# Seven products for the second MLP layer of batch 0, with the w2 sums and batch 1's scaling rearranged around them

## The chip, the cores and the metric

The kernel runs on one core of one Trainium2 chip. A core has TensorE (PE, matrix multiplication; PEld is its loading of weights), VectorE (DVE), ScalarE (ACT) and GpSimd (POOL); SyncE (SP) issues DMA transfers, as POOL does for the weights. The metric is the device time of one execution in microseconds.

## The reference, cut to what matters

```python
# retention, q, k, v: (4, 8, 768, 64); gamma of head h: 1 - 2**(-5 - h)
for t in range(S):
    state = gamma * state + k[:, :, t] (outer) v[:, :, t]
    y[:, :, t] = D**-0.5 * q[:, :, t] @ state
x = y, heads side by side                      # (4, 768, 512)
# mixer
h = x.transpose(0, 2, 1) @ U @ V               # over the 768 tokens, rank 32
u = x + h.transpose(0, 2, 1)
ch = np.maximum(u @ w_ch1, 0.0) @ w_ch2        # 512 -> 2048 -> 512
out = u + ch
```

Inputs and output are fp32; the matmuls here run in bf16.

## The kernel before, in words

For each of four batches the kernel computes retention by chunks of 128 tokens (six chunks), the low-rank mixing, a first MLP layer (512 to 2048, relu) and a second one (2048 to 512). The MLP of batch b and the retention of batch b+1 are woven together: `weave` walks a list of slots (pieces of the two layers, TensorE work of 0.43 to 0.65 us each) and, ahead of each slot, runs the side work that `put` has hung on its number. Every engine executes its instructions in the order in which this program issues them, so the slot numbers fix each engine's queue. `n1` is the number of slots in the first layer (32).

First layer: `mlp1(b, m, hf)` makes one 128-row block m (of 16) of the hidden activation for half hf of the tokens (384 columns), and evicts it with a relu to `gTs[b]`, mostly on ScalarE (L121).

Second layer: batches 1 to 3 use seven products in place of eight (Strassen's scheme) on 2 x 2 blocks. Hidden blocks 0-7 and 8-15 (`lo`, `hi`) and the two token halves give a11, a12, a21, a22; w2's quadrants are b11, b12, b21, b22. `g_sums` (L599) makes five sums of activation blocks on VectorE, `w2_sum` (L589) five of weights (three into `w2s`, two in place). `product` (L620) runs one product for one of three token blocks i: 8 matmuls of 256 columns in two slots, the names in the order 4 5 1 2 3 7 6, accumulated in three PSUM groups A (4, 2, 6), B (5, 3), C (1, 7). `after` (L649) adds the results to `res`: ScalarE copies the partial results of 4, 5, 1 and 2 out of PSUM, POOL makes five sums of them (s5, u1, s1, u2 and later c21), VectorE adds 3, 7 and 6 from PSUM.

Batch 0 instead has `mlp2` (L566): for each of six token chunks one bank, one matmul of V with P and 16 matmuls of 512 columns over all hidden blocks in eight slots, then one add of x on VectorE and one store.

Retention of batch 1, woven into batch 0's second layer: `ret_in` (L275) scales k and q on POOL into `kd` and `qd` (`ret_k`, `ret_q`, L257 and L262) and, for chunks 2 to 4, issues loads of batch 2. `ret_T` (L417) transposes both on TensorE (L424) into one bank and evicts it; `ret_S` makes the scores (two banks for a chunk) and masks them on VectorE (L446); `ret_O` (L450) makes output and state. `at[c]` is the slot of chunk c's transposes, and `ret_in` of c is issued `lead` slots earlier. `mix_P`, `mix_n` (`mix_r` on VectorE, a cast on ScalarE, a DMA transpose) and `mix_u` then make batch 1's mixed input uT, which its first layer reads; they hang on `mix_at`.

The first loads of batch 1 (`gate`) are held back by a small ScalarE instruction in slot 14, so that they come after the weights.

## Time and profile before

| | us |
|---|---|
| median of 3 timed runs (lowest, highest) | 225.2 (224.98, 225.26) |
| the profiled execution's own time | 224.54 |
| its span, first to last instruction | 222.8 |
| PE busy, of the span | 213.7 |
| batch 0, first layer (PE, from the timeline) | 27.43 to 48.31 |
| batch 0, second layer with batch 1's retention | 48.31 to 82.28 |
| VectorE busy / ScalarE busy / POOL busy | 128.1 / 124.9 / 94.2 |

How to read the rows further down. A timeline row has its start, its length, the engine, the line of the kernel, the operation, output<-input, shapes and a count of merged instructions; in brackets stand the engine's idle time ahead of it and what ended it. A matmul's length includes its way through the array, so rows overlap, and the rate is read from start to start. A row of stretches has the stretch, its length, the busy time (and instructions) of PE, PEld, DVE, ACT and POOL, then PE's granted clock, the DMA share and GB/s. A row of a tile or line has its shortest, median and longest duration in ns and its first and last start.

### The profile page before, as it was taken

Reading aid. Unit: us, or ns where it says so; the run is one execution under the profiler, and the core shown is the slowest. Engines: PE = TensorE matmul, PEld = TensorE weight load, DVE = VectorE, ACT = ScalarE, POOL = GpSimd, SP = SyncE. Lnnn points to the kernel's source line nnn. Section 1 sums busy time; section 2 is a strip of 40 time slices with the busy share of each in tenths; the row PEclk is TensorE's granted clock in tenths of the full one; section 3 lists DMA queues with packets and bytes.
Section 4 is the critical chain, followed back from the end, with each engine's and each line's share of the span. In section 5 each row is a group of like instructions: output and inputs, shape, how many; then the busy total and the mean of one; then the engine's idle time right before and its main releaser. Section 6 shows DMA issues by size and latency. Waiting matters only on the chain.

```text
span 222.8 us, 4880 instructions
## 1 busy us (share of the span) xinstructions
PE 213.7 (96%) x1920; PEld 143.3 (64%) x1927; DVE 128.1 (57%) x249; ACT 124.9 (56%) x256; POOL 94.2 (42%) x110
## 2 busy tenths in 40 slices
PE   7898999999999999999999999999999999999991
PEld 2466756554565555566887766657787866668881
DVE  8587640036776456789983721868974423555113
ACT  3377757762327356777445727767454657772220
POOL 6756920039752530614506099423605320006650
PEclk9999999999999999999999999999999999999998
DMA  6999999999999998969499969978621571000222
GB/s 168 245 265 190 154 188 205 199 210 219 201 222 251 228 238 186 222 143 147 94 190 213 234 125 239 179 160 145 83 97 46 121 125 40 0 3 0 94 99 94
DMA packets 100774, 34.89 MB, mean 157 GB/s; under 512 B 87152, under 2 KB 97808, under 8 KB 100752
## 3 DMA queue, kind: packets, MB, share of 16 engines
q1 hardware_dynamic: 94640, 30.29, 66.1%
q0 software_dynamic: 6112, 4.29, 13.1%
q8 instruction: 15, 0.25, 0.5%
q14 instruction: 7, 0.06, 0.1%
HBM read 27.46 MB, written 6.29 MB: 152 GB/s over the span
## 4 chain that ended last, share of the span: by engine, by line
PE 78%; DMA 10%; POOL 3%; DVE 2%; ACT 2%; issue 1%; SPq 1%; POOLq 0%; DVEq 0%; ACTq 0%
PE bk L116 75%; DMA k_n<-in_k_dram 5%; DMA in<-in_q_dram 3%; DMA uT<-x 2%; POOL qd L311 1%; PE bk L424 1%; POOL qd L262 1%; DVE res L661 1%; ACT st L299 1%; POOL s L661 1%; PE bk L318 1%; DVE a L352 1%; POOL kd L306 0%; SPq L166 0%; ACT gT L121 0%
## 5 line engine op out<-in xcount | busy, mean ns | idle before, releaser
L116 PE MATMUL bk<-uT,w1b 128*128 128x384 bf16 x512 | 85.2, 326 | 0.4 <-DMA uT<-x 0.4
L121 ACT ACTIVATE gT<-bk 128x384 bf16<-128x384 f32 x123 | 60.1, 490 | 29.3 <-PE bk L116 29.3
L116 PEld LDWEIGHTS <-w1b 128*128 128x128 bf16 x512 | 49.8, 98 | 33.5 <-issue 0.8
L116 PEld LDWEIGHTS <-gT 128*128 128x128 bf16 x392 | 36.5, 98 | 14.4 <-issue 1.2
L116 PE MATMUL bk<-w2b,gT 128*128 128x256 bf16 (+1 forms) x234 | 43.0, 314 | 0.6 <-ACT s L657 0.2
L257 POOL TENSOR_TENSOR kd<-k_n,Gk 128x512 bf16<-128x512 f32 x18 | 21.7, 1205 | 47.2 <-DMA k_n<-in_k_dram 41.1
L661 POOL TENSOR_TENSOR s<-s,s 128x256 f32<-128x256 f32 x18 | 13.1, 728 | 61.1 <-ACT s L657 55.9
L608 DVE TENSOR_TENSOR gs<-gT 128x768 bf16<-128x768 bf16 x36 | 20.4, 604 | 21.6 <-ACT gT L121 21.3
L446 DVE TENSOR_TENSOR a<-bk,mask 128x512 bf16<-128x512 f32 x36 | 22.7, 682 | 3.8 <-PE bk L116 3.8
L661 DVE TENSOR_TENSOR res<-bk,res 128x256 f32<-128x256 f32 x28 | 10.7, 419 | 21.5 <-PE bk L116 17.0
L262 POOL TENSOR_TENSOR qd<-q_n,Gq 128x512 bf16<-128x512 f32 x18 | 20.3, 1129 | 5.4 <-DMA qkT<-qd 3.6
L116 PEld LDWEIGHTS <-gs 128*128 128x128 bf16 x216 | 20.5, 98 | 3.1
L116 PE MATMUL bk<-w2b,gs 128*128 128x256 bf16 x144 | 19.7, 273 | 0.0
L116 PE MATMUL bk<-w2s,gT 128*128 128x256 bf16 (+1 forms) x152 | 18.5, 267 | 0.0
L657 ACT ACTIVATE s<-bk 128x256 f32<-128x256 f32 x27 | 10.1, 381 | 15.0 <-PE bk L116 14.8
L463 ACT ACTIVATE x<-bk 128x512 bf16<-128x512 f32 x18 | 10.7, 595 | 12.5 <-PE bk L116 9.5
L594 DVE TENSOR_TENSOR w2s<-w2b 128x2048 bf16<-128x2048 bf16 x3 | 5.2, 1783 | 17.1 <-DMA w2b<-in_moe_w_ch_dram 17.1
L533 DVE TENSOR_TENSOR res<-bk,x 128x512 f32<-128x512 f32 x18 | 11.7, 685 | 4.9 <-PE bk L116 4.9
L608 DVE TENSOR_TENSOR gT<-gT 128x768 bf16<-128x768 bf16 x24 | 13.9, 620 | 0.0
L661 POOL TENSOR_TENSOR res<-res,s 128x256 f32<-128x256 f32 x18 | 13.1, 725 | 1.4
L538 ACT ACTIVATE x<-res 128x512 bf16<-128x512 f32 x15 | 9.2, 628 | 6.5 <-DVE res L533 6.2
L482 DVE TENSOR_TENSOR state<-bk,bmask 128x512 bf16<-128x512 f32 x15 | 10.4, 690 | 2.7 <-PE bk L116 2.5
(99 smaller groups left out, 230.9 us busy)
## 6 DMA issues: line engine op xcount, KB each, us to landing
out_dram<-res SPq DMA_DIRECT2D x23, 256.0 KB, 2.7
k_n<-in_k_dram SPq DMA_DIRECT2D x22, 256.0 KB, 4.7
v_n<-in_v_dram SPq DMA_DIRECT2D x22, 256.0 KB, 4.9
q_n<-in_q_dram SPq DMA_DIRECT2D x18, 256.0 KB, 4.9
w2b<-in_moe_w_ch_dram POOLq DMA_DIRECT2D x4, 512.0 KB, 15.2
in<-in_q_dram SPq DMA_DIRECT2D x3, 512.0 KB, 6.3
w1b<-in_moe_w_ch_dram POOLq DMA_DIRECT2D x4, 256.0 KB, 5.5
w1b<-in_moe_w_ch_dram POOLq DMA_DIRECT2D x2, 512.0 KB, 8.6
```

Source lines behind the costliest of these rows:

```text
L116: nc.tensor.matmul(o, l, r, **kw)
L121: nc.scalar.activation(o, i, AF.Relu if relu else AF.Copy)
L257: eng.tensor_tensor(kd, k_n, Gk[:, c].unsqueeze(2).to_broadcast([P, H, D]), op=ALU.mult)
L262: eng.tensor_tensor(qd, rc[b, c]["q_n"], Gq[:, c].unsqueeze(2).to_broadcast([P, H, D]), op=ALU.mult)
L446: nc.vector.tensor_tensor(r["a"][:, e], r["s"][e].rearrange("p (n t) -> p n t", n=NP), mask4, op=ALU.mult)
L463: nc.scalar.activation(x_of(b, c), o, AF.Copy)
L482: nc.vector.tensor_tensor(sb, ps.rearrange("p (n t) -> p n t", n=NP), bmask4, op=ALU.mult)
L533: nc.vector.tensor_tensor(res_of(b, j), h, xs[b, j], op=ALU.add)
L538: nc.scalar.activation(xs[b, j], res[b, j], AF.Copy)
L608: nc.vector.tensor_tensor(o, x, y, op=op)
L657: nc.scalar.activation(t[nm], o, AF.Copy)
L661: eng.tensor_tensor(o, x, y, op=op)
```

## The change

Batch 0's second layer now runs as the seven products too, and `mlp2` is gone. For this:

- The six products of V with P (`mix_r(0, j)`) move into batch 0's first layer, slots 4 to 15.
- The first layer of batch 0 makes hidden blocks in the order 0, 1, 8, 9, 2, 3, 10, 11, and so on; w1's pieces and w2's four pieces are loaded in that order of use.
- `g_sums(0, n)` come at slots 9, 17, 25 and at the layer's end. `w2_sum` works on halves (four hidden blocks of eight) and makes all ten sums in batch 0: five at slot 22, two at slot 30, three at the layer's end, between the last five activation sums. The two that stood in batch 1 are gone from there.
- Batch 1's scaling and transposes are hung on later slots (`at` = n1 + 11, 14, 18, 22, 26, 30, before n1 + 7, 12, 17, 22, 27, 32), its scores by single chunks, its mixing at n1 + 36 (of 42 slots, before n1 + 38 of 48).
- PSUM: batch 0's products use three banks; batch 1's first layer begins with four.

```diff
-    def mlp2(b, j, part, of):
-        if part == 0:
-            chp[b, j] = mm_bank()
-            matmul(chp[b, j], Vb[:, ts(j, P)], Ps[b], DM, start=True, stop=False)
-        ch = chp[b, j]
-        for m in range(part * NM // of, (part + 1) * NM // of):
-            matmul(ch, gTs[b][:, m, ts(j, P)], w2b[:, m], DM, start=False, stop=(m == NM - 1))
-        if part == of - 1:
-            o = res_of(b, j)
-            nc.vector.tensor_tensor(o, chp.pop((b, j)), xs[b, j], op=ALU.add)
...
-    def w2_sum(i):
-        b11, b12, b21, b22 = w2_quads()
-        o, x, y, op = ((w2s[:, 0], b11, b22, ALU.add), (w2s[:, 1], b11, b12, ALU.add),
-                       (w2s[:, 2], b21, b22, ALU.add), (b12, b12, b22, ALU.subtract),
-                       (b21, b21, b11, ALU.subtract))[i]
+    def w2_sum(i, h):
+        b11, b12, b21, b22 = (x[:, ts(h, HM // 2)] for x in w2_quads())
+        z = w2s[:, :, ts(h, HM // 2)]
+        o, x, y, op = ((z[:, 2], b21, b22, ALU.add), (b21, b21, b11, ALU.subtract),
+                       (z[:, 0], b11, b22, ALU.add), (z[:, 1], b11, b12, ALU.add),
+                       (b12, b12, b22, ALU.subtract))[i]
         nc.vector.tensor_tensor(o, x, y, op=op)
...
     def mlp1_slots(b):
         if b == 0:
-            return [lambda m=m, hf=hf: mlp1(b, m, hf) for m in range(NM) for hf in (0, 1)]
+            ms = [m + x for m in range(0, HM, 2) for x in (0, 1, HM, HM + 1)]
+            return [lambda m=m, hf=hf: mlp1(b, m, hf) for m in ms for hf in (0, 1)]
...
-            for i in range(3):
-                put(side, n1 + 1 + i, lambda i=i: w2_sum(i))
-            at, lead, mix_at = [n1 + 7 + 5 * c for c in range(NCK)], 4, n1 + 38
-            S_at = {(0, 1): n1 + 14, (2, 3): n1 + 24, (4,): n1 + 30, (5,): n1 + 35}
-            O_at = [n1 + i for i in (19, 22, 29, 32, 35, 38)]
+            for j, i in enumerate((4, 6, 8, 13, 14, 15)):
+                put(side, i, lambda j=j: mix_r(0, j))
+            for n, i in enumerate((9, 17, 25)):
+                put(side, i, lambda n=n: g_sums(0, n))
+            for i in range(5):
+                put(side, 22, lambda i=i: w2_sum(i, 0))
+            for i in (0, 1):
+                put(side, n1 - 2, lambda i=i: w2_sum(i, 1))
+            for f, *args in ((g_sums, 0, 3, (0, 1)), (w2_sum, 2, 1), (g_sums, 0, 3, (2,)),
+                             (w2_sum, 3, 1), (w2_sum, 4, 1), (g_sums, 0, 3, (3, 4))):
+                put(side, n1, lambda f=f, args=args: f(*args))
+            at, lead, mix_at = [n1 + i for i in (11, 14, 18, 22, 26, 30)], 4, n1 + 36
+            S_at = {(c,): n1 + i for c, i in enumerate((14, 17, 21, 25, 29, 33))}
+            O_at = [n1 + i for i in (18, 21, 25, 29, 33, 36)]
         if b == 1:
...
-            for n, i in enumerate((3, 4)):
-                put(side, 2 + 3 * n, lambda i=i: w2_sum(i))
...
         if b and nxt:
-            set_banks([0, 1, 2])
+            set_banks([0, 1, 2, TP])
+            put(side, 22, lambda: set_banks([0, 1, 2]))
...
-            put(side, mix_at, lambda: use.update(mix=[2, SA, SB, OB] if b == 0 else [SA, SB, OB]))
+            put(side, mix_at, lambda: use.update(mix=[SA, SB, OB] + [TP] * (b == 0)))
```

POOL's queue from the start of batch 0's second layer, before (kd_1_c and qd_1_c are the scaled k and q of batch 1's chunk c):

```order
L257 TENSOR_TENSOR kd_1_0_888<-k_n_1_0_730,Gk_157 128x512
L262 TENSOR_TENSOR qd_1_0_890<-q_n_1_0_733,Gq_156 128x512
L257 TENSOR_TENSOR kd_1_1_916<-k_n_1_1_736,Gk_157 128x512
L262 TENSOR_TENSOR qd_1_1_918<-q_n_1_1_738,Gq_156 128x512
L257 TENSOR_TENSOR kd_1_2_943<-k_n_1_2_740,Gk_157 128x512
L262 TENSOR_TENSOR qd_1_2_945<-q_n_1_2_742,Gq_156 128x512
```

And now (s4, s5, s1 and c21 are the copied partial results of products 4, 5, 1 and 2, res_0_j the output of batch 0's chunk j):

```order
L646 TENSOR_TENSOR s5_952<-s4_941,s5_952 128x256
L646 TENSOR_TENSOR res_0_0_669<-res_0_0_669,s5_952 128x256
L646 TENSOR_TENSOR s1_965<-s1_965,s5_952 128x256
L646 TENSOR_TENSOR res_0_3_744<-res_0_3_744,s1_965 128x256
L257 TENSOR_TENSOR kd_1_0_973<-k_n_1_0_752,Gk_157 128x512
L262 TENSOR_TENSOR qd_1_0_975<-q_n_1_0_755,Gq_156 128x512
L646 TENSOR_TENSOR res_0_3_744<-res_0_3_744,c21_981 128x256
L257 TENSOR_TENSOR kd_1_1_994<-k_n_1_1_758,Gk_157 128x512
L262 TENSOR_TENSOR qd_1_1_996<-q_n_1_1_760,Gq_156 128x512
```

Four sums of the first token block now stand ahead of chunk 0's scaling, and one more ahead of chunk 1's. On TensorE the transposes of chunk 0 stand after 11 of the 14 slots of that block.

VectorE's queue at the end of batch 0's first layer and behind it, before:

```order
L123 TENSOR_SCALAR gT_0_639<-bk6_55_655 128x384
L594 TENSOR_TENSOR w2s_191<-w2b_97 128x2048 x3
L576 TENSOR_TENSOR res_0_0_913<-bk1_84_877,x_0_0_395 128x512
L125 COPY qkT_1_1_939<-bk3_87_930 128x1024
L446 TENSOR_TENSOR a_1_0_975<-bk4_88_955,mask_175 128x512
```

and now:

```order
L578 TENSOR_TENSOR w2s_191<-w2b_97 128x1024
L578 TENSOR_TENSOR w2b_97<-w2b_97 128x4x256
L593 TENSOR_TENSOR gs_0_712<-gT_0_639 128x768 x2
L578 TENSOR_TENSOR w2s_191<-w2b_97 128x1024
L593 TENSOR_TENSOR gs_0_712<-gT_0_639 128x768
L578 TENSOR_TENSOR w2s_191<-w2b_97 128x1024
L578 TENSOR_TENSOR w2b_97<-w2b_97 128x4x256
L593 TENSOR_TENSOR gT_0_639<-gT_0_639 128x2x384 x2
L646 TENSOR_TENSOR res_0_0_669<-bk2_91_943,res_0_0_669 128x256
L646 TENSOR_TENSOR res_0_3_744<-bk2_91_943,res_0_3_744 128x256
```

Where three sums of w2 stood, there are now the last five half sums of w2 and the last five sums of the activation, in the order in which the products use them.

The end of batch 0's second layer on VectorE (res_1_j belongs to `mix_n` of batch 1's chunk j), before:

```order
L533 TENSOR_TENSOR res_1_3_1320<-bk4_116_1318,x_1_3_1224 128x512
L533 TENSOR_TENSOR res_1_4_1328<-bk5_117_1326,x_1_4_1268 128x512
L533 TENSOR_TENSOR res_1_5_1336<-bk6_118_1334,x_1_5_1291 128x512
L576 TENSOR_TENSOR res_0_5_1358<-bk0_115_1310,x_0_5_580 128x512
L125 CAST uT_1_1309<-bk6_122_1367 128x384
```

and now:

```order
L533 TENSOR_TENSOR res_1_3_1487<-bk5_125_1485,x_1_3_1340 128x512
L646 TENSOR_TENSOR res_0_5_803<-res_0_5_803,bk0_113_1305 128x256
L533 TENSOR_TENSOR res_1_4_1499<-bk6_126_1497,x_1_4_1413 128x512
L533 TENSOR_TENSOR res_1_5_1505<-bk3_127_1503,x_1_5_1449 128x512
L125 CAST uT_1_1470<-bk6_130_1521 128x384
```

The last add of batch 0's output now stands between the adds of chunks 3 and 4. On TensorE the matmuls for chunks 4 and 5 and for uT come behind the last slot; before, five slots lay between the first of them and the next layer.

More of the change, by code (lines that the diff above doesn't have):

```diff
@@ L822 @@
                          lambda: mlp1_two(0, (0, 1), 1), lambda: None]
-            for i, s in ((1, 2), (2, 3)):
-                put(side, i, lambda s=s: load_w1(512 * s, 512))
-            for s in range(4):
-                put(side, 4 + s, lambda s=s: load_w2(s))
+            for i, s in ((1, 512), (2, DH // 2 + 512)):
+                put(side, i, lambda s=s: load_w1(s, 512))
+            for n, s in enumerate((0, 2, 1, 3)):
+                put(side, 4 + n, lambda s=s: load_w2(s))
             for c, nm in ((0, "kq"), (1, "kq"), (2, "kq"), (0, "v"), (3, "kq"), (1, "v"), (4, "kq"),
```

30 lines of the change are left out of this document (12 added, 18 removed).

## The prediction

> **What bounds the kernel now.** I read first the page's busy shares, then the busy time by stretches, then TensorE's own timeline through batch 0.
>
> ```profile
> PE 213.7 (96%) x1920; PEld 143.3 (64%) x1927; DVE 128.1 (57%) x249; ACT 124.9 (56%) x256; POOL 94.2 (42%) x110
> 30.00:40.00 10.00, 10.00 (x63) 6.02 (x62) 0.56 (x1) 7.50 (x18) 0.00 (x0) 1.00 1.23 204
> 50.00:60.00 10.00, 9.41 (x76) 4.85 (x76) 7.58 (x9) 2.39 (x3) 9.07 (x8) 1.00 1.03 209
> ```
>
> PE is busy 96% of the span. In the stretches the columns are PE, PEld, DVE, ACT, POOL, then the granted clock. From 30 to 40 us VectorE and POOL stand almost empty; from 50 to 60 us POOL is busy 9.07 us of 10, and that is where the change puts more work on POOL.
>
> ```profile
> 27.43 21.05 PE L116 MATMUL bk<-uT,w1b 128*128 128x384 bf16 x128
> 48.31 0.38 PE L116 MATMUL bk<-P_sb,Vb 128*128 128x512 bf16 x1
> 52.14 0.40 PE L424 MATMUL bk<-ident,qd 128*128 128x128 bf16 x4 [0.43 <-POOL qd L262]
> ...
> 69.56 0.39 PE L424 MATMUL bk<-ident,qd 128*128 128x128 bf16 x4
> 70.00 0.39 PE L116 MATMUL bk<-state,qkT 128*128 128x128 bf16 x4
> 70.68 0.38 PE L116 MATMUL bk<-P_sb,Vb 128*128 128x512 bf16 x1
> 70.90 1.46 PE L116 MATMUL bk<-w2b,gT 128*128 128x512 bf16 x6
> 72.29 0.40 PE L116 MATMUL bk<-qkT 64*128 64x128 bf16 x8
> 72.62 0.40 PE L116 MATMUL bk<-state,qkT 128*128 128x128 bf16 x4
> 82.28 4.06 PE L116 MATMUL bk<-uT,w1b 128*128 128x384 bf16 x24
> ...
> 212.64 1.04 PE L116 MATMUL bk<-w2b,gs 128*128 128x256 bf16 x8
> 213.51 1.04 PE L116 MATMUL bk<-w2s,gs 128*128 128x256 bf16 x8
> ```
>
> Batch 0's first layer starts at 27.43, its second layer (with batch 1's retention woven in) at 48.31, batch 1's first layer at 82.28. The one wait of note in between is 0.43 us at 52.14: the first transposes of batch 1 waited for POOL's qd. Starts of neighbouring rows give unit costs: a 512-column matmul 0.22 us (70.68 to 70.90), a product's 8 matmuls of 256 columns 0.87 (212.64 to 213.51), the transposes T of a chunk 0.44 (69.56 to 70.00), its output part O 0.68 (70.00 to 70.68; chunks 0 and 5 do less, 0.46), its scores S 0.43 (six 512s from 70.90 end at 72.19; the next stage starts at 72.62). A slot of the second layer costs 0.43 in both kernels (2 x 512 or 4 x 256 columns).
>
> **PE's work.** The layer had 96 x 512 columns and gets 168 x 256: 96 x 0.2165 = 20.8 against 21 x 0.87 = 18.3, so **-2.5 us**. The six products with V stay, but move into the first layer: 6 x 0.22, so that layer ends at 48.31 + 1.3 = **49.6**. Their VectorE adds meet an engine that was idle there (0.56 us of work from 30 to 40 us), and cost nothing. Scores by chunk cost 6 x 0.43, about what two pairs and two singles took.
>
> **The sums on VectorE.** Their inputs first.
>
> ```profile
> L157 POOL DMA_DIRECT2D w2b<-in_moe_w_ch_dram x4: 777/792/805, 26.5 to 28.7; - x4
> DMA to landing us min/median/max: 12.3/15.2/19.1
> L594 DVE TENSOR_TENSOR w2b<-w2b x2: 1215/1216/1216, 84.3 to 85.4; 128x2048 bf16<-128x2048 bf16 x2
> L608 DVE TENSOR_TENSOR gs<-gT x36: 545/552/1393, 91.5 to 200.7; 128x768 bf16<-128x768 bf16 x36
> ```
>
> The last piece of w2 lands at 28.7 + 19.1 = 47.8. 2048 elements take 1.216 us and 768 take 0.55, so 1024 take about 0.68, with 0.6 from start to start. The sums over the first half of w2 and the third part of gT (five of 0.6, five of 0.47) run from 42 to 48 us beside the first layer. The next two half sums then run from 47.8 to 49.1, before product 4 reaches the second half of w2 at 50.0: covered. From the last eviction (50.3, 0.7 behind the last matmul) VectorE has four sums in a row (0.5 + 0.65 + 0.5 + 0.65) until 52.5, then three more. Product 3, due at 53.1, wants its half sum of b12 at 53.5; with POOL between (next part) it comes at 53.9: **+0.4**. Without the load of w2 in time (it would have to land 1 us later) product 4 would wait too; this is in the range. Batch 1 loses two w2 sums on VectorE, where nothing waited for them: nothing gained.
>
> **The scaling, behind the sums on POOL.** This is the main term. Durations:
>
> ```profile
> 213.77 0.38 ACT L657 ACTIVATE s<-bk 128x256 f32<-128x256 f32 x1 [0.49 <-PE bk L116]
> 214.23 0.72 POOL L661 TENSOR_TENSOR s<-s,s 128x256 f32<-128x256 f32 x1 [2.41 <-ACT s L657]
> ...
> 118.30 0.73 POOL L661 TENSOR_TENSOR s<-s,s 128x256 f32<-128x256 f32 x1 [6.43 <-ACT s L657]
> 119.10 0.73 POOL L661 TENSOR_TENSOR res<-res,s 128x256 f32<-128x256 f32 x1
> 119.79 0.72 POOL L661 TENSOR_TENSOR s<-s,s 128x256 f32<-128x256 f32 x1
> ...
> 131.85 1.04 POOL L257 TENSOR_TENSOR kd<-k_n,Gk 128x512 bf16<-128x512 f32 x1
> 132.85 1.04 POOL L262 TENSOR_TENSOR qd<-q_n,Gq 128x512 bf16<-128x512 f32 x1
> ```
>
> A POOL sum follows its product's end by 0.72 (product ends 213.51, POOL starts 214.23) and takes 0.75 from start to start; a scaling takes 1.00. In the new queue kd and qd of chunk 0 stand behind four sums of the first token block. Product 5 ends at 49.6 + 2 x 0.87 = 51.3, so POOL starts at 52.05, and qd is done at 52.05 + 4 x 0.75 + 2 x 1.0 = 57.1 if nothing disturbs it. Before, the two scalings started at 48.21, when k landed. What disturbs it:
>
> ```profile
> 47.98 1.23 DVE L594 TENSOR_TENSOR w2s<-w2b 128x2048 bf16<-128x2048 bf16 x1 [17.11 <-DMA w2b<-in_moe_w_ch_dram]
> 48.21 1.89 POOL L257 TENSOR_TENSOR kd<-k_n,Gk 128x512 bf16<-128x512 f32 x1 [18.70 <-DMA k_n<-in_k_dram]
> 49.12 2.06 DVE L594 TENSOR_TENSOR w2s<-w2b 128x2048 bf16<-128x2048 bf16 x1
> 50.08 2.01 POOL L262 TENSOR_TENSOR qd<-q_n,Gq 128x512 bf16<-128x512 f32 x1
> 51.11 2.06 DVE L594 TENSOR_TENSOR w2s<-w2b 128x2048 bf16<-128x2048 bf16 x1
> 52.05 2.02 POOL L257 TENSOR_TENSOR kd<-k_n,Gk 128x512 bf16<-128x512 f32 x1
> ```
>
> POOL's 1.04 becomes 2.0 and VectorE's 1.22 becomes 2.06, each as long as one of its own and one of the other's: while VectorE sums two SBUF tensors the two run by turns. So POOL's start waits for the sum that VectorE is in (until 52.5), and the last three VectorE sums (0.6 + 0.47 + 0.47) slip between POOL's: 57.1 + 0.45 + 1.5 = **59.0**.
>
> PE comes to chunk 0's transposes after 11 slots: 49.6 + 11 x 0.435 + 0.4 = 54.8. It waits **4.2 us** (2.7 without the turns, when product 3 doesn't wait either). The transposes sit in PE's queue ahead of the rest of product 7, so all products queue behind them. From there POOL's queue stays ahead of PE's by lateness: chunk 1 (one sum, two scalings) 59.0 + 2.75 = 61.75, PE there at 59.0 + 0.44 + 3 x 0.43 + 0.43 = 61.2: **+0.6**. Chunk 2 fits. Chunk 3's scaling stands behind two sums that need product 5 of the next block (copied at 64.95): 65.0 + 1.5 + 2.0 = 68.5, PE at 68.05: **+0.45**. Chunk 4 has three sums ahead: 68.5 + 2.25 + 2.0 = 72.75, PE at 68.5 + 0.44 + 3 slots + S + O + a slot = 71.8: **+0.9**. Chunk 5 fits (74.75 against 76.1). Loads are no part of it: k and q of chunk 0 land by 50.08 as before, the later ones are issued from the same queue position, and batch 2's loads, which follow chunks 2 to 4 on the DMA queue behind two output stores, are needed only in batch 1.
>
> **The tail.** Batch 1's mixing moves to the end of the layer.
>
> ```profile
> 78.57 2.06 DVE L533 TENSOR_TENSOR res<-bk,x 128x512 f32<-128x512 f32 x3 [1.61 <-PE bk L116]
> 79.29 1.99 ACT L538 ACTIVATE x<-res 128x512 bf16<-128x512 f32 x3 [1.93 <-DVE res L533]
> 81.19 1.44 ACT L121 ACTIVATE uT<-bk 128x384 bf16<-128x384 f32 x3
> 81.95 0.33 PE L116 MATMUL bk<-ident,x 128*128 128x128 bf16 x3
> ```
>
> Before, five slots of products lay between the mixing's matmuls and hid this chain: three adds on VectorE, three casts on ScalarE, and only behind them the evictions of uT that batch 1's first layer reads. In the new order two of the three adds' matmuls and all of uT's come after the last slot, at a time I call E. VectorE's adds then end at E + 0.46, + 1.5 and + 2.2 (a sum for the output in between), ScalarE's last cast at + 2.85, its first two uT evictions at + 3.3 and + 3.75. PE, done with the mixing at E + 1.75 (2 x 0.22 and 4 x 0.33, the row at 81.95), can start the second matmul of the layer only at + 3.8, so the layer runs as from + 3.65: **+1.9**. From qd of chunk 4 to E lie 11.3 us of PE work, so E = 84.05 and batch 1 starts as from 87.7, against 82.28. Of PE's idle time in the old kernel (222.8 - 213.7 = 9.1 us) 4.7 lie behind its last matmul and most of the rest before 27 us, so nothing later can give the shift back.
>
> **Sum.** -2.5 (columns) - 0.45 (the old wait) + 0.4 + 4.2 + 0.6 + 0.45 + 0.9 + 1.9 = **+5.5 us**. It is made against the profiled execution (224.54 us, its span 222.8); the median of the timed runs is 225.2, so I predict **230.7**.
>
> **Bounds.** Without the turns all from chunk 0 on comes 1.9 earlier: +3.6. With the tail's chain hidden, another 1.9 less: +1.7, the far low end. On the other side stands the clock.
>
> ```profile
> 1.19 6.27 PE L116 MATMUL bk<-idle 128*128 128x512 bf16 x18 [1.19 <-DVE idle L180]
> ...
> 218.00:219.00 1.00, 0.06 (x2) 0.00 (x0) 1.00 (x5) 0.00 (x0) 0.00 (x0) 1.00 0.08 27
> 220.00:221.00 1.00, 0.00 (x0) 0.00 (x0) 0.00 (x0) 0.00 (x0) 0.00 (x0) 0.87 0.95 318
> 221.00:222.00 1.00, 0.00 (x0) 0.00 (x0) 0.00 (x0) 0.00 (x0) 0.00 (x0) 0.50 0.12 33
> ```
>
> PE's last matmul ends at 218.06, and the granted clock falls to 0.50 at about 220.74 (0.87 of that microsecond): 2.7 us of an idle PE were enough once. And a cold start costs: the kernel's first 18 matmuls of 512 columns took 6.27 us where 18 x 0.2165 is 3.9.
>
> **Rivals.** *The clock falls in the new wait.* A gap of 4.2 us is longer than 2.7. At half speed the 2.17 us from 59.0 to chunk 1's transposes take 4.35 (2.2 lost; the start lost 2.4); they come at 63.35, not 61.75, and what follows on POOL follows PE: +1.6, so **232.3**. For it: the gap's length. Against: one gap only, and its length hangs on the turns. By the Trainium skill (TensorE: Matmul & The Clock Gate, "What's actually happening") the clock halves after a whole idle window of about 3.4 us in a free-running raster; by that rule a 4.2 us gap holds a whole window in one phase of four, my estimate. The trace's 2.7 us is shorter than the page's window.
>
> *The cheap case.* VectorE is done with its sums before POOL starts, so there are no turns: +3.6, **228.8**. It decides if VectorE ends by 52.05, 2 us earlier than its own work alone gives (54.1); nothing in the rows says so.
>
> *Not slower.* POOL's sums hold its queue for 0.35 us or less, the 0.72 being mostly latency that the next instruction overlaps. Then qd of chunk 0 is done at 52.05 + 1.4 + 2.0 = 55.45, PE waits 1.05 there, chunks 1 to 4 fit (ten sums and ten scalings take 13.5 us from 52.05, not 17.5 and the turns), and with the tail's 1.9 the change breaks even: **225.2**. Against it: POOL sums at 118.30, 119.10 and 119.79 started 0.80 and 0.69 apart, though copies for all of them were there.
>
> That the change moves nothing of this is excluded by POOL's order, in which the sums stand ahead of the scaling.
>
> **How the numbers follow.** The forecast has 0.52, the clock 0.25, the cheap case 0.18, not slower 0.05. The range takes in the first three with the low bound's tail in part: **228.0 to 233.0**; the forecast's own range is 229.5 to 231.5. A measurement of this kernel tells 0.2% from no change: faster 0.03, same 0.02, slower 0.95.
>
> **What would show it.** In the new profile: transposes of line 424 idle about 4 us for POOL's qd near 55 us; POOL rows of 0.72 grown to about 1.3 from 52 to 57; shorter waits at chunks 1, 3 and 4; a gap of about 2 us before batch 1's first layer, released by ScalarE's uT; PE's granted clock below 1.00 near 59 us or not. No POOL wait at the transposes, or a first layer of batch 1 that starts before 84 us, would prove the forecast wrong.

## The result and the profile after

| | before | after |
|---|---|---|
| median of 4 timed runs (lowest, highest), us | 225.23 (224.98, 225.77) | 231.26 (230.28, 231.46) |
| profiled execution: time / span / PE's mean granted clock | 224.54 / 222.8 / 0.995 | 230.28 / 228.5 / 0.986 |
| batch 0, second layer starts (PE) | 48.31 | 49.66 |
| batch 1, first layer starts (PE) | 82.28 | 87.93 |
| from there to the end of the span | 140.5 | 140.6 |

The changed kernel takes 1.0256 of the time before, 95% interval 1.022 to 1.0291. The last two rows of the table place the loss: it is complete when batch 1's first layer starts, and nothing behind that gives it back. A ratio compares fast runs alone: one run of e14 further down, 1.6% above the fastest of its kernel, counts as slow and is in that row's median but not in its ratio.

The profiled execution of the changed kernel, 230.28 us, is the fastest of its four (the others took 231.07 to 231.46). All rows below are from it, so about 1 us of the difference between the medians is in no row.

The page of the changed kernel: busy shares, and the ten microseconds in which POOL was nearly full before.

```profile
PE 215.0 (94%) x1997; PEld 151.2 (66%) x1999; DVE 143.2 (63%) x287; ACT 128.4 (56%) x267; POOL 102.6 (45%) x125
...
50.00:60.00 10.00, 6.40 (x55) 5.25 (x53) 6.38 (x10) 2.43 (x6) 7.76 (x9) 0.92 1.01 212
```

From 50 to 60 us PE works 6.40 of 10 us (9.41 before) at a mean clock of 0.92, VectorE 6.38 (2.39 before). Note that POOL shows *less* work than before, 7.76 against 9.07, because it now starts only when the first copies of products reach it; yet it is POOL that PE waits for. A busy share says nothing of when an engine is ready.

PE's timeline of the changed kernel, from product 3 to batch 1:

```profile
53.15 1.24 PE L116 MATMUL bk<-w2b,gT 128*128 128x256 bf16 x8
54.23 0.60 PE L116 MATMUL bk<-w2s,gT 128*128 128x256 bf16 x4
58.38 0.61 PE L424 MATMUL bk<-ident,qd 128*128 128x128 bf16 x4 [3.55 <-POOL qd L262]
...
62.22 0.40 PE L424 MATMUL bk<-ident,qd 128*128 128x128 bf16 x4
...
69.18 0.40 PE L424 MATMUL bk<-ident,qd 128*128 128x128 bf16 x4 [0.39 <-POOL qd L262]
73.36 0.40 PE L424 MATMUL bk<-ident,qd 128*128 128x128 bf16 x4 [0.70 <-POOL qd L262]
...
84.42 0.60 PE L116 MATMUL bk<-w2s,gT 128*128 128x256 bf16 x4
...
87.93 4.28 PE L116 MATMUL bk<-uT,w1b 128*128 128x384 bf16 x24 [0.55 <-ACT uT L121]
```

The four matmuls at 54.23 end their share of PE at 54.23 + 4 x 0.109 = 54.67, so the transposes of chunk 0 come 3.71 us late (the row's 3.55 counts from the modelled end of the last matmul, 0.16 later). The same 0.16 belongs to the other waits: 0.55 us at chunk 3, 0.86 at chunk 4. The last slot of the second layer ends at 84.42 + 0.44 = 84.86.

POOL's timeline of the changed kernel over the same stretch:

```profile
52.08 1.12 POOL L646 TENSOR_TENSOR s<-s,s 128x256 f32<-128x256 f32 x1 [22.41 <-DVE gs L593]
53.28 1.05 POOL L646 TENSOR_TENSOR res<-res,s 128x256 f32<-128x256 f32 x1
54.30 1.03 POOL L646 TENSOR_TENSOR s<-s,s 128x256 f32<-128x256 f32 x1
55.41 0.92 POOL L646 TENSOR_TENSOR res<-res,s 128x256 f32<-128x256 f32 x1
56.29 1.04 POOL L257 TENSOR_TENSOR kd<-k_n,Gk 128x512 bf16<-128x512 f32 x1
57.29 1.04 POOL L262 TENSOR_TENSOR qd<-q_n,Gq 128x512 bf16<-128x512 f32 x1
...
59.97 1.04 POOL L262 TENSOR_TENSOR qd<-q_n,Gq 128x512 bf16<-128x512 f32 x1
```

And VectorE's there:

```profile
51.93 0.69 DVE L578 TENSOR_TENSOR w2s<-w2b 128x1024 bf16<-128x1024 bf16 x1
52.65 1.10 DVE L578 TENSOR_TENSOR w2b<-w2b 128x1024 bf16<-128x1024 bf16 x1
53.67 2.07 DVE L593 TENSOR_TENSOR gT<-gT 128x768 bf16<-128x768 bf16 x2
55.67 0.41 DVE L646 TENSOR_TENSOR res<-bk,res 128x256 f32<-128x256 f32 x1
```

POOL's four sums stand ahead of chunk 0's scaling and take 1.12, 1.05, 1.03 and 0.92 us where one alone takes 0.72. VectorE's sums beside them grow as well: 1.10 for a half sum of w2, where the one that had started just ahead of POOL's first sum took 0.69, and 1.03 each for two that alone take 0.55. VectorE's add at 55.67, which reads PSUM, keeps its 0.41.

The clock of the changed kernel, microsecond by microsecond (the number behind POOL's busy time):

```profile
58.00:59.00 1.00, 0.62 (x7) 0.62 (x7) 0.00 (x0) 0.00 (x0) 1.00 (x3) 0.70 0.65 134
59.00:60.00 1.00, 1.00 (x8) 0.81 (x7) 0.00 (x0) 0.54 (x1) 1.00 (x3) 0.50 0.97 217
60.00:61.00 1.00, 1.00 (x7) 0.69 (x6) 0.42 (x1) 0.48 (x1) 1.00 (x3) 0.50 0.94 212
61.00:62.00 1.00, 1.00 (x9) 0.49 (x9) 0.01 (x1) 0.00 (x0) 1.00 (x3) 0.60 0.78 176
```

The clock fell just as PE resumed and stayed at half for (0.30 + 0.50 + 0.50 + 0.40) / 0.50 = 3.4 us. Chunk 1's transposes, for which POOL was ready at 61.0 (59.97 + 1.04), came at 62.22 with no wait.

### The profile page after: what moved, and what is told of

It reads as the page before. It is cut to its first block, busy times and chain, and to the rows that moved or that the text cites. A ratio compares the mean times of both kernels' runs of the same rounds, so it can differ in the third digit from the quotient of the medians.

```text
span 228.5 us, 5097 instructions
## 1 busy us (share of the span) xinstructions
PE 215.0 (94%) x1997; PEld 151.2 (66%) x1999; DVE 143.2 (63%) x287; ACT 128.4 (56%) x267; POOL 102.6 (45%) x125
## 4 chain that ended last, share of the span: by engine, by line
PE 63%; POOL 11%; issue 10%; DMA 4%; DVE 4%; ACT 3%; SPq 3%; POOLq 0%; DVEq 0%; ACTq 0%
PE bk L116 61%; POOL s L646 4%; POOL res L646 4%; DMA k_n<-in_k_dram 2%; POOL qd L262 2%; DMA q_n<-in_q_dram 2%; SPq L288 2%; POOL kd L257 1%; SPq L136 1%; PE bk L424 1%; DVE a L352 1%; ACT st L299 1%; DVE res L646 1%; ACT x L538 1%; ACT kT L299 1%
## 5 line engine op out<-in xcount | busy, mean ns | idle before, releaser
L646 POOL TENSOR_TENSOR s<-s,s 128x256 f32<-128x256 f32 x24 | 18.2, 758 | 87.5 <-ACT s L642 65.1
L593 DVE TENSOR_TENSOR gs<-gT 128x768 bf16<-128x768 bf16 x48 | 27.7, 614 | 20.8 <-ACT gT L121 20.3
L116 PEld LDWEIGHTS <-gs 128*128 128x128 bf16 x288 | 27.3, 98 | 3.9
L116 PE MATMUL bk<-w2b,gT 128*128 128x256 bf16 x192 | 26.4, 273 | 0.1
L116 PE MATMUL bk<-w2b,gs 128*128 128x256 bf16 x192 | 26.2, 273 | 0.0
L116 PE MATMUL bk<-w2s,gT 128*128 128x256 bf16 (+1 forms) x200 | 26.2, 277 | 0.0
L646 POOL TENSOR_TENSOR res<-res,s 128x256 f32<-128x256 f32 x24 | 17.9, 747 | 1.9
L593 DVE TENSOR_TENSOR gT<-gT 128x768 bf16<-128x768 bf16 x32 | 18.2, 609 | 0.0
L116 PE MATMUL bk<-w2s,gs 128*128 128x256 bf16 x96 | 12.6, 273 | 0.0
L116 PEld LDWEIGHTS <-qkT 64*128 64x128 bf16 (+1 forms) x204 | 8.4, 95 | 4.7 <-issue 2.9
```

The lines of the kernel that those rows point to most:

```text
L116: nc.tensor.matmul(o, l, r, **kw)
L593: nc.vector.tensor_tensor(o, x, y, op=op)
L646: eng.tensor_tensor(o, x, y, op=op)
```

## The experiments

They ran on four chips (e1, e4, e5, e6 on one; e7 to e10 on a second; e11 to e13 on a third; e14 on a fourth), each time with the kernel before beside them (medians 224.66 to 224.93 us). A ratio is to that kernel. The changed kernel itself was not repeated there; its 1.0256 is the mark, and as its interval is 1.022 to 1.0291, the ratios of e5 to e9 and of e13 are not clear of it: what these runs show is in their rows. "Start" is PE's first row of batch 1's first layer in the profiled run (before 82.28, changed kernel 87.93). Batch 0's first layer starts at 27.29 to 27.50 us in these profiles, so 0.2 us between two starts mean nothing.

| run | edit | median us | ratio, 95% | start |
|---|---|---|---|---|
| e1_scale_first | chunks 0 and 1 scaled ahead of the sums | 228.78 | 1.0178 (1.0155, 1.0202) | 86.29 |
| e4_tail | uT's evictions ahead of the casts | 232.10 | 1.0324 (1.0297, 1.0351) | 87.30 |
| e5_fill | 16 idle matmuls ahead of chunk 0's transposes | 229.45 | 1.0209 (1.0181, 1.0237) | 86.58 |
| e6_no_turns | last three VectorE sums left out | 229.52 | 1.0216 (1.0182, 1.0249) | 85.81 |
| e7_no_pool_sums | batch 0's POOL sums left out | 229.86 | 1.0208 (1.0143, 1.0273) | 87.96 |
| e8_rearranged | both kinds of sums reordered | 229.39 | 1.0220 (1.0155, 1.0286) | 86.83 |
| e9_tail_part | uT's evictions between the casts | 231.21 | 1.0286 (1.0249, 1.0324) | 86.74 |
| e10_no_sums | e6 and e7 together | 227.02 | 1.0113 (1.0055, 1.0171) | 85.07 |
| e11_adds_later | e8, with adds and sums in the order of use | 226.14 | 1.0059 (1.0030, 1.0088) | 82.77 |
| e12_and_mix_earlier | e11, mixing two slots earlier | 226.02 | 1.0060 (1.0041, 1.0078) | 82.94 |
| e13_mix_earlier | mixing two slots earlier, alone | 231.43 | 1.0292 (1.0254, 1.0330) | 87.61 |
| e14_by_block | e11, last activation sums cut finer | 229.33 | 1.0151 (1.0116, 1.0186) | 87.32 |

**Is the wait POOL's order?** (e1_scale_first)

```diff
-            put(side, max(0, at[c] - lead), lambda c=c: ret_in(b, c))
+            put(side, at[0] - 11 if b == 1 and c < 2 else max(0, at[c] - lead),
+                lambda c=c: ret_in(b, c))
```

> The scaling of chunks 0 and 1 is put at the end of the first layer, so on POOL it stands ahead of the sums of products 5, 1 and 2. Theory (queue order and turns together): the wait at the first transposes of batch 1 (3.6 us) goes and the clock stays at 1.00, but VectorE's last sums now take turns with four scalings, so products 1 to 3 wait 2 to 4 us in all; chunk 4's transposes come some 4 us earlier than 73.4: 227.0 to 228.5 us. Rival (the queue order alone, turns cost little): the products don't wait, chunk 4's transposes come 6 us earlier: 225 us. Rival (neither: PE waits for something else there): 231 us.

PE's row with the largest wait in e1_scale_first, and chunk 0's transposes:

```profile
54.12 0.87 PE L116 MATMUL bk<-w2s,gs 128*128 128x256 bf16 x4 [1.93 <-DVE w2s L578]
...
58.40 0.39 PE L424 MATMUL bk<-ident,qd 128*128 128x128 bf16 x4
```

VectorE's rows ahead of it:

```profile
49.91 2.71 DVE L593 TENSOR_TENSOR gs<-gT 128x768 bf16<-128x768 bf16 x2
52.54 1.52 DVE L578 TENSOR_TENSOR w2s<-w2b 128x1024 bf16<-128x1024 bf16 x1
```

The transposes of chunk 0 no longer wait: the order on POOL was the cause. But the wait did not vanish, it changed sides. The scaling now runs from 48.25 us beside VectorE's sums, which grow to 1.36 and 1.52 us each, and product 1 waits 1.93 us for its half sum of w2. Chunk 4's transposes and batch 1's start come 1.64 us earlier than in the changed kernel, where 4 were expected, and the clock, which was to stay at 1.00, fell for 3.4 us (rows in the last section). The ratio lies above the theory (228.5 against 225.23 would be 1.0145) and below the rival's 231 us.

**What do the turns cost, and what the clock?** e6 leaves out a half sum of b12 and two activation sums; e5 lets PE run empty matmuls through the wait:

```diff
-                             (w2_sum, 3, 1), (w2_sum, 4, 1), (g_sums, 0, 3, (3, 4))):
+                             (w2_sum, 3, 1)):
...
+            for cost in (0.65, 0.55, 0.55):
+                put(side, n1, lambda cost=cost: bal.book("V", cost))
```

(The last two lines only keep the program's bookkeeping of VectorE's work as it was.)

```diff
+    def fill(n):
+        w = bank(TP)
+        for _ in range(n):
+            nc.tensor.matmul(w, idle[:, :P], idle, start=True, stop=True)
...
+            if b == 0:
+                put(side, at[0], lambda: fill(16))
```

> Left out: the last three sums on VectorE in batch 0, all in place (the second half of b12 - b22 and the last part of a12 - a22 and a11 - a21). Theory (turns): POOL's sums from 52.6 to 55.5 us run undisturbed, the first qd is done at 57.5, not 58.3, and product 3 doesn't wait: 230.3 us; 229.2 if the wait is then too short for the clock to fall. Rival (no turns, VectorE's sums don't matter to POOL): qd at 58.3, 231.3 us.

> Sixteen idle matmuls (3.5 us) stand on PE in front of the first transposes of batch 1, inside the wait; nothing else moves. Theory (the fall of the clock costs on top of the wait): the granted clock stays at 1.00 from 58 to 62 us, the second transposes come at 61.1, not 62.2, and all behind them: 230.1 us. Rival (POOL sets the pace there, so the clock costs nothing): granted clock 1.00, but 231.3 us.

POOL's second sum in e6_no_turns, and PE's row at chunk 0:

```profile
53.16 0.72 POOL L646 TENSOR_TENSOR res<-res,s 128x256 f32<-128x256 f32 x1
...
57.42 0.40 PE L424 MATMUL bk<-ident,qd 128*128 128x128 bf16 x4 [2.91 <-POOL qd L262]
```

And at chunks 0 and 1 in e5_fill, where line 424 has become 429:

```profile
58.19 0.40 PE L429 MATMUL bk<-ident,qd 128*128 128x128 bf16 x4
...
60.88 0.40 PE L429 MATMUL bk<-ident,qd 128*128 128x128 bf16 x4 [0.43 <-POOL qd L267]
```

Without the last VectorE sums POOL's sums behind its first take 0.72 us again, and chunk 0's transposes come at 57.42, not 58.38. Of these 0.96 us 0.12 lie ahead of batch 0's first layer, so the turns of the three sums cost some 0.84 us there. In e5 the transposes come at 58.19, nearly as late as in the changed kernel, but the clock stays at 1.00 and chunk 1 comes 2.69 us behind chunk 0, not 3.84. So the fall of the clock costs some 1.15 us in the profiled run, and the wait as such the rest; batch 1 starts 1.35 us earlier, 0.19 of it from ahead of the first layer. Across the timed runs this price doesn't stand out. A piece of 3.4 us at half clock brings the mean clock of a run of 229 us to 0.993 or less; one of the changed kernel's runs had a mean of 0.996 and took 231.07 us, no less than the others, and e1's three runs with 0.995 to 0.999 took 228.63 to 229.0 beside 228.55 with 0.989. What they lost instead no trace shows. In e6 the clock did not fall either, with an idle gap of 2.91 us. (Part of e6's gain is lost again at 132.5 us; see below.)

**Is it the sums at all?** e7 leaves out the 15 POOL sums of batch 0's products, e10 these and e6's three:

```diff
         def on(eng, o, x, y, op):
+            if b == 0 and eng is nc.gpsimd:
+                return
             eng.tensor_tensor(o, x, y, op=op)
```

> Leaves out the 15 GpSimd sums of batch 0's products (s4, s5, s1, c21 are still copied), so batch 0's output is not complete. Theory (queue and turns): GpSimd's scaling of chunks 0 and 1 runs from 48.2 us on, as soon as k and q land, as in e1_scale_first; the transposes find qd ready, chunks 3 and 4 do not wait. But the scaling now takes turns with VectorE's sums, so product 3 or its neighbours wait 1.5 to 2 us for w2s or gs as in e1. Ratio to before 1.011 to 1.016. Rival (the sums on GpSimd alone cost everything, the turns nothing): no wait at all in batch 0's second layer, ratio 0.997 to 1.003. Rival (the transposes are late for another reason than GpSimd's queue): ratio 1.022 or more.

> Leaves out the 15 GpSimd sums of batch 0's products and the last three VectorE sums of batch 0's first layer (a half sum of b12 and two sums of the last activation blocks), so the output is wrong in all batches. Theory: neither queue nor turns are left; PE runs through batch 0's second layer with waits below 0.5 us in all and full clock, and only the tail (1.5 us) stands against the 2.5 us of columns: span before 222.8 - 2.5 - 0.45 + 1.5 = 221.4, ratio 0.994 to 1.002 with up to 1 us for waits that open later. Rival (something else in the new layer costs, such as the order of the first layer or the scores by chunk): ratio above 1.006.

PE's two large waits in e7_no_pool_sums:

```profile
54.41 0.60 PE L116 MATMUL bk<-w2s,gs 128*128 128x256 bf16 x4 [1.93 <-DVE w2s L578]
58.62 1.01 PE L116 MATMUL bk<-w2b,gT 128*128 128x256 bf16 x4 [1.62 <-DVE w2b L578]
```

VectorE's rows of the same run:

```profile
50.20 2.71 DVE L593 TENSOR_TENSOR gs<-gT 128x768 bf16<-128x768 bf16 x2
52.83 1.52 DVE L578 TENSOR_TENSOR w2s<-w2b 128x1024 bf16<-128x1024 bf16 x1
...
57.16 1.41 DVE L578 TENSOR_TENSOR w2b<-w2b 128x1024 bf16<-128x1024 bf16 x1
```

This is the clearest picture of the turns. With its sums gone POOL scales four chunks from 48.5 to 59.5 us without a pause, and every VectorE sum takes 1.36 to 1.52 us whatever its own 0.55 or 0.69. PE waits 1.93 us for product 1's and 1.62 us for product 3's weights: the second of these was not expected, and the clock fell for 6.8 us in the profiled run, so the ratio (four runs from 227.48 to 230.72 us) is above what the theory said, though their intervals meet, while the wait's place and kind are the theory's. The one run whose mean clock, 0.997, leaves no room for a fall took 227.48 us, 1.012 of the kernel before, as the theory has it. That the POOL sums alone cost everything is excluded. e10 missed its theory and came out where its rival stood (above 1.006, for something else in the new layer). PE's largest wait in its second layer, though, is again 1.93 us for product 1's half sum of w2: leaving both kinds of sums out was said to leave no turns, and it left the scaling against the sums that remained. The expectation had overlooked what e1 had shown: the scaling takes turns too.

**Can the order be mended?** e8 scales chunk 0 ahead of all sums, chunk 1 behind two, chunk 3 ahead of the second block's, and makes the last activation sums for the first block's 128 columns first (`g_sums` takes the first column and their number as two more arguments):

```diff
-            for f, *args in ((g_sums, 0, 3, (0, 1)), (w2_sum, 2, 1), (g_sums, 0, 3, (2,)),
-                             (w2_sum, 3, 1), (w2_sum, 4, 1), (g_sums, 0, 3, (3, 4))):
+            for f, *args in ((g_sums, 0, 3, (0, 1), 2, 0, P), (w2_sum, 2, 1),
+                             (g_sums, 0, 3, (2,), 2, 0, P), (w2_sum, 3, 1), (w2_sum, 4, 1),
+                             (g_sums, 0, 3, (3, 4), 2, 0, P), (g_sums, 0, 3, range(5), 2, P, 2 * P)):
...
-            put(side, max(0, at[c] - lead), lambda c=c: ret_in(b, c))
+            i = NM * 2 + (0, 4, 14, 15, 18, 26)[c] if b == 1 else max(0, at[c] - lead)
+            put(side, i, lambda c=c: ret_in(b, c))
```

> Same arithmetic in another order: chunk 0 of batch 1 is scaled on GpSimd ahead of all sums, chunk 1 behind two sums, chunk 3 ahead of the second block's sums, chunk 4 behind two of them; the last activation sums of batch 0 are made for the first 128 columns first, the other 256 columns behind the w2 sums. Theory: the wait at the transposes is gone, product 3 waits at most 0.7 us, chunk 2 at most 0.5, the clock stays at 1.00, the tail stays: -2.5 - 0.45 + 1.5 + 0.5 to 1.5, ratio 0.996 to 1.003. Rival (the turns move the wait to product 3 and the clock falls anyhow, as in e1_scale_first): 1.010 to 1.018.

PE's rows in e8_rearranged: the transposes of chunks 0 and 1, then the second block's first product:

```profile
54.92 0.39 PE L424 MATMUL bk<-ident,qd 128*128 128x128 bf16 x4
57.11 0.40 PE L424 MATMUL bk<-ident,qd 128*128 128x128 bf16 x4
61.46 1.38 PE L116 MATMUL bk<-w2b,gT 128*128 128x256 bf16 x8 [3.73 <-DVE res L647]
```

VectorE's rows of the same run (L594 are the activation sums there, L647 the adds of products):

```profile
55.71 2.99 DVE L594 TENSOR_TENSOR gs<-gT 128x512 bf16<-128x512 bf16 x3
58.62 2.12 DVE L594 TENSOR_TENSOR gT<-gT 128x512 bf16<-128x512 bf16 x2
60.66 1.07 DVE L647 TENSOR_TENSOR res<-bk,res 128x256 f32<-128x256 f32 x3
```

Up to 57.1 us this is what was wanted: chunks 0 and 1 are transposed without a wait. Then PE stands 3.73 us, because VectorE's adds, which free PSUM for the second block, now stand behind five sums that take turns. The wait moved, as the rival had it, but to another place; the ratio's interval reaches from the rival's range to well above it. e11 puts the adds first, and holds GpSimd's two adds to the lower rows, with the store of these rows, back until behind them:

```diff
-                             (g_sums, 0, 3, (3, 4), 2, 0, P), (g_sums, 0, 3, range(5), 2, P, 2 * P)):
+                             (g_sums, 0, 3, (3, 4), 2, 0, P)):
...
+            for i, which in ((10, (0, 1)), (15, (2, 3, 4))):
+                put(side, n1 + i, lambda which=which: g_sums(0, 3, which, 2, P, 2 * P))
+            put(side, n1 + 15, lambda: [f() for f in held])
...
+        hold = held.append if b == 0 and i == 0 else lambda f: f()
...
-            on(nc.gpsimd, u2[:, n2], u2[:, n2], t["s1"], ALU.add)
+            hold(lambda: on(nc.gpsimd, u2[:, n2], u2[:, n2], t["s1"], ALU.add))
...
-                on(nc.gpsimd, u2[:, n1], u2[:, n1], t["c21"], ALU.add)
+                hold(lambda: on(nc.gpsimd, u2[:, n1], u2[:, n1], t["c21"], ALU.add))
...
-            i = NM * 2 + (0, 4, 14, 15, 18, 26)[c] if b == 1 else max(0, at[c] - lead)
+            i = NM * 2 + (0, 4, 10, 14, 20, 26)[c] if b == 1 else max(0, at[c] - lead)
```

> As e8_rearranged, but VectorE's adds of products 3, 7 and 6 of the first block no longer stand behind GpSimd's adds to the same rows nor behind all the sums over the other 256 columns: GpSimd's two adds to the lower rows come after VectorE's, the five sums over the 256 columns stand in two pieces (behind product 3's adds, and ahead of the second block), chunk 2 is scaled ahead of those two adds. Theory (VectorE's and GpSimd's sums share one way and must be ordered by use): no wait of PE above 0.7 us from 49.6 us to the tail, clock 1.00, transposes of chunk 2 near 60 and of chunk 3 near 64 us; -2.5 - 0.45 + 1.5 of tail + 0.5 to 1: ratio 0.994 to 0.998, up to 1.004 with waits that open at the end of batch 1. Rival (the shared work of some 15 us from 48 us on cannot be hidden in any order): a wait of 2 us or more at another place and ratio 1.010 or more.

PE's rows in e11_adds_later:

```profile
54.44 0.39 PE L424 MATMUL bk<-ident,qd 128*128 128x128 bf16 x4
...
59.26 0.38 PE L116 MATMUL bk<-qkT 64*128 64x128 bf16 x7 [0.38 <-DVE a L446]
...
82.77 4.28 PE L116 MATMUL bk<-uT,w1b 128*128 128x384 bf16 x24 [0.55 <-ACT uT L121]
```

No row of PE in the second layer has more than 0.4 us of idle time, the clock stays at 1.00 there, and batch 1 starts at 82.77: some 5 of the 5.65 us are back by order alone, with the same arithmetic. The ratio, 1.0059 (1.0030, 1.0088), is above the theory's 0.994 to 0.998, its interval touching the 1.004 that waits at the end of batch 1 were to explain; the twelve runs go from 224.72 to 227.1 us. The columns saved are still spent on the tail and on four waits for VectorE's masks and state: 1.1 us by the rows' idle time, and 1.9 us if the stretch from 57.95 to 63.99 us is set against the same matmuls in the changed kernel (63.55 to 67.73).

e14 tried to make VectorE's part cheaper by cutting the sums that delay those masks to half their columns (256 elements a row in place of 512), the other half later:

```diff
-            for i, which in ((10, (0, 1)), (15, (2, 3, 4))):
-                put(side, n1 + i, lambda which=which: g_sums(0, 3, which, 2, P, 2 * P))
+            for i, j, which in ((10, 1, (0, 1)), (15, 1, (2, 3, 4)), (23, 2, range(5))):
+                put(side, n1 + i, lambda j=j, which=which: g_sums(0, 3, which, 2, j * P, P))
```

> e11_adds_later with the last activation sums cut to the use: columns 128 to 255 where all 256 stood, columns 256 to 383 eight slots later (slot n1 + 23). Theory: VectorE's sums between 55.9 and 61.8 us halve, so the masks come in time and the 1.1 us of waits at the scores of chunks 1 and 2 (and at chunk 1's output) fall to 0.4 or less: ratio 0.998 to 1.004 against 1.0059. Rival (the last sums, moved to 66 us, delay the masks of chunk 3 or an add there, or the gain opens as a wait at the end of batch 1): ratio 1.004 to 1.009.

VectorE's rows in e14_by_block, the first with POOL idle, the second beside it:

```profile
51.79 0.28 DVE L594 TENSOR_TENSOR gs<-gT 128x256 bf16<-128x256 bf16 x1
...
59.36 2.17 DVE L594 TENSOR_TENSOR gT<-gT 128x256 bf16<-128x256 bf16 x2
```

PE's largest wait of the same run (L650 are adds of products there):

```profile
71.52 0.60 PE L116 MATMUL bk<-w2b,gT 128*128 128x256 bf16 x4 [1.61 <-DVE res L650]
```

A miss that teaches most. Beside a busy POOL a sum of 256 elements takes 1.09 us, where one of 512 took 1.22 in e11 (2.44 for two) and one of 256 alone takes 0.28: most of it is POOL's instruction. Halving the size saved 0.13 us a sum and the five added sums (from 66.4 to 70.8 us) cost a turn each, so that VectorE's adds came late again, by 1.61 us at 71.5, and the clock fell once more. (The new bookings also put one eviction of qkT on VectorE, for another wait of 0.96 us at 63.4, and PE waits 1.27 us for a copy of ScalarE at 134.3, as in the next runs; the ratio contains both. Two runs with a mean clock of 0.996 and 0.998, which leaves no room for a fall, took 228.0 and 227.9 us, so e14 is slower than e11 without the fall too.)

**The tail.** Four runs tried to shorten the chain of adds, casts and evictions ahead of batch 1's first layer: e4 with all of uT's evictions ahead of the casts, e9 with two of them between casts, e13 and e12 with the mixing two slots earlier (n1 + 34 for n1 + 36) in the changed kernel and in e11.

```diff
-            put(side, i + 5 + n, lambda j=j: mix_n(b, j))
+            put(side, i + 5 + n + (b == 1), lambda j=j: mix_n(b, j))
...
-                put(side, i + 5 + len(js) + c, lambda c=c: mix_u(b, 0, c))
+                put(side, i + 5, lambda c=c: mix_u(b, 0, c))
```

```diff
             put(side, i + 5 + n, lambda j=j: mix_n(b, j))
-        if b == 1:
-            for c in range(NCB):
-                put(side, i + 5 + len(js) + c, lambda c=c: mix_u(b, 0, c))
+            for c in ((0, 1), (2, 3), ())[n] if b == 1 else ():
+                put(side, i + 5 + n, lambda c=c: mix_u(b, 0, c))
```

> Only the tail of batch 0 changes: uT's matmuls and evictions for chunks 0 to 2 come ahead of the adds and casts of chunks 3 to 5. Theory: batch 1's first layer no longer waits for ScalarE's evictions (0.55 us at its first matmul, about as much at the second, 0.2 at the mixing), so 1.0 to 1.5 us less: 229.8 to 230.3 us. Rival (the transposes of chunks 3 to 5 now come too late for the second half of the tokens): no gain, 231 us, with a wait for the DMA of uT some 6 us into batch 1's first layer.

> At the end of batch 0 the first two pieces of uT are evicted between the casts of chunks 3 and 4, the other two between those of chunks 4 and 5. Theory: batch 1's first layer can start 0.6 to 1.2 us earlier and the transposes of the casts come later by two evictions (0.9 us), which its order of blocks still covers: ratio 0.003 to 0.005 below the changed kernel's 1.0256, so 1.020 to 1.023. Rival (as in e4_tail the time is lost again at the transposed half): 1.025 to 1.032.

> The changed kernel with batch 1's mixing two slots earlier and nothing else. Theory: the 1.5 us of tail shrinks by 0.5 to 0.9 us, ratio 1.021 to 1.0235 against 1.0256. Rival (as in e9_tail_part the gain is taken back at the end of batch 1): 1.025 to 1.031.

> e11_adds_later with batch 1's mixing two slots earlier (mix_at n1 + 34). Theory (the tail is a fixed chain behind the mixing's first matmuls): batch 1's first layer starts 0.5 to 0.9 us earlier than in e11_adds_later, and SyncE's transposes with it: ratio 0.990 to 0.999. Rival (the gain opens as a wait at the end of batch 1, for ScalarE's s or for uT): within 0.002 of e11_adds_later.

PE's rows in e4_tail:

```profile
94.11 0.82 PE L116 MATMUL bk<-uT,w1b 128*128 128x384 bf16 x4 [0.94 <-DMA uT<-x]
...
135.88 1.03 PE L116 MATMUL bk<-w2b,gT 128*128 128x256 bf16 x8 [1.64 <-ACT s L642]
```

All four miss their theories; the ratios of e9, e12 and e13 lie where their rivals put them, and e4's lies above its rival's. In e4 and e9 the wait for ScalarE's uT is gone (batch 1 starts at 86.74 in e9; at 87.30 in e4, whose clock was low for 6.8 us in the profiled run), but in e4 the transposed half of uT is then late by 0.94 us, and in both profiled runs PE waits about 1.6 us at the end of batch 1, e4's 1.64 at 135.88 and a 1.54 of the same kind in e9. e13 moves the start by 0.3 us against the changed kernel, e12 by 0.2 the other way against e11 (0.18 of it lies ahead of batch 0's first layer), and neither changes the time measurably. So the tail's 1.5 us is there, but none of these ways gets it back. The waits at the end of batch 1 differ between the profiled runs without a clear rule (before 0.17 and 0.36 us, the changed kernel, e1, e8 and e11 none, e6 0.94, e10 0.77 and 1.44, e12 0.36 and 0.90, e14 1.27); in e4 ScalarE's copy stood behind a cast whose add on VectorE had waited 1.84 us for a store of the output. What decides their size was not settled, and the ratios of the runs named contain them.

## Why the prediction was right, and where not

The forecast of 230.7 us, its direction and its place hold. By its own terms, from the profiled run (a wait is the time lost, the row's idle time and 0.16):

| term of the sum | predicted | measured |
|---|---|---|
| first layer ends | 49.6 | 49.66 |
| product 3 waits | 0.4 | 0.2 (its eight matmuls take 1.24 instead of 1.04) |
| chunk 0's transposes wait for qd | 4.2 | 3.71 |
| chunk 1 | 0.6 | 1.67 (62.22 instead of 58.38 + 2.17) |
| chunk 3 | 0.45 | 0.55 |
| chunk 4 | 0.9 | 0.86 |
| tail | 1.9 | 1.54 (88.15 against 84.86 + 1.75 of mixing) |

- **Columns and old wait (-2.95).** No row shows it by itself. Taken over, it makes the measured terms add up to 5.6 us, and batch 1's first layer runs 5.9 us later (as from 88.15, its first 24 matmuls taking 4.28 us where before they took 4.06). So what the other terms leave for it is about -2.7.
- **Chunk 0.** Queue and turns are shown, by e1 (order) and e6 (some 0.84 us less at the transposes). The size was 0.5 too large: the four POOL sums were put at 4.5 us from 52.5 (57.0) with their turns and ended at 56.3, since POOL could begin at 52.08 and the sums slowed to 0.92 to 1.12 us, not 1.3. That the transposes would wait as long as POOL's chain says, ahead of the rest of product 7, is as predicted.
- **Chunk 1: the step that failed.** "The forecast" was the case without a fall of the clock, with the fall as a rival at +1.6 us and a chance of 0.25. The clock did fall in the profiled run, in the microsecond in which PE resumed, and chunk 1 came 1.2 us after POOL had its qd ready; the forecast's own 0.6 us for POOL would have been 0.5. e5 confirms the size (1.15 us between the two chunks), which is below the rival's 1.6. So the rival's mechanism ran on top of the forecast's, while the waits were 0.5 + 0.2 us and the tail 0.4 us smaller than predicted: in the profiled run the sum was met by luck, because two errors of about 1.1 us cancel. For the median, 231.26 us, this balance is not shown: the other three runs took about 1 us more than the profiled one, one of them with no room for the fall.
- **The rule on the clock.** By the Trainium skill (TensorE: Matmul & The Clock Gate, "What's actually happening") a whole idle window of about 3.4 us halves the clock. By that rule a gap only little longer should do it in few phases, which is an estimate. By the rows' idle times, the gap of 3.55 us did it here, and so did those of 3.55 in e4, e9 and e13 and of 3.73 in e8, while e6's of 2.91 us did not; but e1's and e10's of 1.93 and e14's of 1.61 did. The runs do not support a gap of 3.4 us as the condition.
- **The cheap case** (no turns, 228.8) and **not slower** (POOL's sums hold its queue 0.35 us or less) are excluded by POOL's rows: 0.92 to 1.12 us each, one right behind the other.
- **Turns.** That VectorE and POOL alternate was right, but used too narrowly: the prediction charged it to VectorE's last four sums, which meet POOL's first four. e1, e7, e8, e10 and e14 show that all of POOL's work and VectorE's two-operand sums on SBUF from 48 us on forms one queue. In it stand VectorE's ten sums (five of 0.69, five of 0.55: 6.2 us) and POOL's five sums and scaling of chunks 0 to 2 (5 x 0.73 + 6 x 1.04 = 9.9 us). That is an estimate of 16 us, less what each pair hides, to be passed between 48 and 60 us. PE needs parts of both, so moving either ahead only moves the wait. By the Trainium skill (SBUF — State Buffer, "SBUF: two separate sides") the pair of ports that VectorE and GpSimd share is locked for a whole instruction. The rows agree in the alternation, down to PSUM adds that are not slowed (0.41 beside POOL); a pair of scaling and sum takes some 0.23 us less than the two alone (last section).
- **Nothing later gives it back.** Right: 140.5 and 140.6 us from batch 1's first layer to the end.

No run beat the kernel before. The best, e11 and e12, are 0.6% slower; in e11's profile what the seven products save is spent on the tail (1.5 us) and on waits for VectorE (some 2.0 us, 0.1 of it at product 3).

## What to carry to other kernels

Before work is put on an engine that "has room", look which other engine it shares a way into memory with, and add up the two queues over the stretch in which both must finish: here some 16 us of work wanted one way in 12 us, and only an order by use (adds that free PSUM first, then what PE needs next, then the rest) hid most of it. On a shared way the number of instructions can count more than their size, so cutting work finer can make it worse (e14). And price a new idle gap of PE twice, once for its length and once for the clock that may fall behind it.
